# A smaller first place for the experts, and tokens fetched ahead of weights

## The chip, the cores and the metric

The kernel runs on one core of a Trainium2 chip. The metric is the device time of one execution in microseconds (us). Before the change the median of three timed runs is 489.94 us (487.93 to 490.13). The trace that is read below is of one more execution, which took 488.21 us.

## What is computed

Three stages follow each other: causal attention with a decay, for 2 batches of 8 heads and 576 positions; a mixture of eight experts, where each token goes to the expert with the highest logit and an expert takes at most 288 tokens; and one more two-layer network.

```python
x = attention(q, k, v, f)                 # 1152 tokens of 512
logits = x @ w_gate; expert_idx = np.argmax(logits, axis=1)
for i in range(N):                        # in order, at most 288 per expert
    e = expert_idx[i]
    if counts[e] < capacity: disp[e, counts[e]] = x[i]; ...
h = np.maximum(np.einsum('ecd,edf->ecf', disp, w1), 0.0)
y = np.einsum('ecf,efd->ecd', h, w2)
out[i] = gate_w[i] * y[expert_idx[i], pos[i]]
h2 = out @ w_in; g = piecewise(h2); return g @ w_out
```

With the inputs of these runs expert 0 gets 89 tokens and the other seven 69 to 288.

## The kernel before

**Attention** goes over 16 heads in steps of about 5 us. TensorE (PE) works on scores of one head and on the product with V of another; ScalarE (ACT) takes the exponentials into `pt`; GpSimd (POOL) masks their diagonal blocks (`affine_select`, L542), and PE's product with V (`av_part`, L579) needs the masked blocks. The order of each step is a list written by hand (`ORDER`).

**Dispatch.** `disp` in DRAM has E times `CAPS` rows: a slot per expert and position. SP fills it with zeros (L880), two transfers of 128 rows at the start of each step, 22 in all. From step 11 on POOL scatters the scaled token rows into it (L720, `scatter`): five scatters for the first batch, inside the last steps of attention, and five for the second batch after attention. `CAPS` is worked out from the table `PLACES`: the largest place but one with an overflow area `RW` behind it, where `RW` is the largest number of tokens by which an expert may exceed its place.

**Places.** The experts are not run by number, but by place: `PLACES` gives for each of the eight places the rank of the expert by its token count and the rows that the place computes. Place 0 is always expert 0, and its tokens don't come from `disp`: PE picks them with selection matrices (`pick` on VectorE (DVE), `perm` on PE, L712: ten token tiles by four column blocks, 40 products, each two records in the trace) straight into `XT`. What exceeds a place is done later under `tc.If` (`rest`); with these inputs no place is exceeded.

**One place** has 8 weight quarters of 512 KB: four of `w1`, four of `w2`. PE goes over 8 column blocks `fc` of `w1` (L1035 where the place has up to 160 rows, in plain fp32), and ACT's Relu (L1090) moves each from one of four PSUM banks into `hf`. Then the `w2` half follows in eight parts. Places over 160 rows (2, 4, 6) are "split": weights and tokens are made into a high and a low half first, and PE takes three products (L991 to L993). For place 2 the splitting of the tokens stands inside the `w1` loop of place 1: `x_trans` is called after blocks 1, 3, 5 and 7. Its DVE transpose (L1020) reads the fetched tokens, and its ACT copy (L1021) stands in ACT's queue ahead of the Relu of blocks 2 and 3.

**Loads.** All weights come over SP's queue in one order, `loads`; `pump` (L189) issues the next as soon as one of 13 buffers (8 `RAW`, 5 `ST`) is free. The eight quarters of place 0 are loaded in attention. `x_fetch(e)` puts four transfers (L400) for the tokens of place `e` into the same queue, out of `disp`, so it waits for the scatters. SP carries its list out in order.

Of the kernel before, what the change touches and what calls it, by code (L numbers as in the profile page):

```python
# [10 lines left out]
F32 = mybir.dt.float32  # L11
# [4 lines left out]
ACTF = mybir.ActivationFunctionType  # L16
# [8 lines left out]
def most_over(places, n):  # L25
    best = 0
    for m in range(1 << len(places)):
        over = [p for p in range(len(places)) if m >> p & 1]
        need = sum(places[p][1] + 1 for p in over if p == 0)
        for r in range(len(places) - 1):  # L30
            need += max([places[p][1] + 1 for p in over if p and places[p][0] >= r], default=0)
        if need <= n:
            best = max(best, len(over))
    return best
# [3 lines left out]
def attention_moe_mlp_kernel(  # L38
# [14 lines left out]
    nc = tc.nc  # L53
# [6 lines left out]
    KD = DM // 128  # L60
# [3 lines left out]
    KF = 8  # L64
# [1 line left out]
    NG = 3  # L66
    GW = N // NG
    GT = GW // 128
    PLACES = ((7, 160), (6, 128), (0, 288), (5, 128), (1, 224), (4, 128), (2, 192), (3, 160))
    CP = [c for _, c in PLACES]  # L70
    C0, CMAX = CP[0], max(CP)
    PS = [sum(CP[:p]) for p in range(E + 1)]
    LEFT = [min(cap, N // (r + 1) if p else N) - c for p, (r, c) in enumerate(PLACES)]
    RW = max(LEFT) // 32 * 32
    CAPS = max([c + RW for c, o in zip(CP, LEFT) if o > 0] + CP)
    NK = most_over(PLACES, N)
    XW = max([min(N, PS[p]) + CP[p] for p in range(E)] + [N + RW])
    THREE = 256
    SPLIT = [c > 160 for _, c in PLACES]
    NHL = 5  # L80
# [19 lines left out]
    xt_p = ctx.enter_context(tc.tile_pool(name="xtp", bufs=1))  # L100
# [25 lines left out]
    def build_consts(pos_c):  # L126
# [5 lines left out]
        for e in range(E):  # L132
            nc.gpsimd.memset(slot_c[:, e:e + 1], float(e * CAPS) - BIG)
            nc.gpsimd.memset(rev_c[:, e:e + 1], float(E - e))
            nc.gpsimd.memset(tie_c[:, e:e + 1], float(E - e if e else -E * N))
            nc.gpsimd.memset(place_c[:, e], float(PLACES[e][0]))
            nc.gpsimd.memset(cap_c[:, e:e + 1], float(CP[e]))
# [10 lines left out]
    def quarter_src(i):  # L148
        p, r = divmod(i, 8)
        w = (w1, w2)[r // 4]  # L150
        if p == 0:
            return w1[E, r] if r < 4 else w2[0, r - 4]
        return w[bass.ds(at_place(p), 1), r % 4].rearrange("e p f -> (e p) f")
# [3 lines left out]
    def at_place(p):  # L157
        if p not in places:
            places[p] = nc.sync.value_load(ord_i[0:1, p:p + 1], min_val=0, max_val=E - 1)
        return places[p]  # L160
# [18 lines left out]
    def pump(n=99):  # L179
        while n and free and loads:  # L180
            _, kind, i = loads.popleft()
            t = raws[kind, i] = free.popleft()
            if kind == "w":
                src = quarter_src(i)
            elif kind == "m":
                t, src = t.bitcast(U32), (w_in, w_out)[i % 2][i // 2].bitcast(U32)
            else:
                src = more_src(i)
            nc.sync.dma_start(out=t, in_=src)  # L189
            n -= 1  # L190
# [200 lines left out]
        nc.vector.tensor_tensor(out=order_sb, in0=ps[:, NT:], in1=ge[:, 0, 0:NT], op=ALU.add)  # L391

    xrs, xts, x_next = {}, {}, []
    XT = xt_p.tile([128, KD, C0], F32, tag="xt", name="XT")

    def x_load(e, src):
        n = src.shape[0] // 32
        xrs[e] = x_next[e % 2]
        for j in range(DM // 128):
            nc.sync.dma_start(out=xrs[e][32 * j:32 * j + 32, 0:n],  # L400
                          in_=src[:, 128 * j:128 * j + 128].rearrange("(t p) d -> p t d", p=32))


    with ExitStack() as actx:
# [303 lines left out]
        def perm(b, ibs, ks=range(KD)):  # L708
            for ib in ibs:
                n = min(128, S - ib * 128)  # L710
                for k in ks:
                    nc.tensor.matmul(px[k][:, 0:C0], xss[b][:n, ib, 2 * k:2 * k + 2].rearrange("p h d -> p (h d)"),  # L712
                                     sel[b, ib][:n].bitcast(F32), start=((b, ib) == (0, 0)),
                                     stop=((b, ib) == (NB - 1, IB - 1)))

        def scatter(b, ibs):
            si, xs = sis[b], xss[b]
            for ib in ibs:
                n = min(128, S - ib * 128)
                nc.gpsimd.indirect_dma_start(  # L720
                    out=disp_v[b * IB + ib], out_offset=bass.IndirectOffsetOnAxis(ap=si[:n, ib:ib + 1], axis=0),
                    in_=xs[:n, ib].rearrange("p h d -> p (h d)"), in_offset=None,
                    bounds_check=E * CAPS - 1, oob_is_err=False)
# [149 lines left out]
        for t in range(-AHD, NH + 1):  # L873
# [24 lines left out]
            if t == HB + 6:  # L898
                px = [next(s1), next(s1), next(s2), next(s2)]
# [21 lines left out]
        for k in range(KD):  # L921
            perm(1, range(3, IB), (k,))
        xts[0] = XT
        for k in range(KD):
            if k % 2:
                nc.vector.tensor_copy(out=XT[:, k], in_=px[k][:, 0:C0])
            else:
                nc.scalar.activation(out=XT[:, k], in_=px[k][:, 0:C0], func=ACTF.Copy)
        scatter(1, range(IB))
        bases_gen = compact_bases()  # L930

# [34 lines left out]
    def m_step(h):  # L966
        while m_at and m_at[0] <= h:
            m_at.pop(0)
            next(conv)
# [32 lines left out]
    with ExitStack() as mctx:  # L1002
        mp = mctx.enter_context(tc.tile_pool(name="moe", bufs=1))
        x_next.extend(mp.tile([128, max(CP[2 - i::2] + [RW]) // 32, 128], F32, name=f"xn_r{i}")
                      for i in range(2))
        xn = mp.tile([128, KD, 2, CMAX], F32R, name="xn")
        hf = mp.tile([128, KF, C0], F32, name="hf")
        xT0 = mp.tile([128, CMAX], F32, name="xT0")

        def x_trans(e, k, n, split):  # L1010
            if k == 0:
                xts[e] = xn if split else XT
            x = xts[e][:, k]
# [15 lines left out]
        def bank(ring, n, split):  # L1029
            t = next(ring)  # L1030
            return t[:, 0:n] if n >= THREE or not split else t[:, 0:2 * n].rearrange("p (z c) -> p z c", c=n)

        def product(ps, w, c, a, first, last):
            if len(a) == 1:
                nc.tensor.matmul(ps, w[:, c], a[0], start=first, stop=last)  # L1035
            elif len(ps.shape) == 2:
                three(ps, w[:, 0, c], w[:, 1, c], a[0], a[1], first, last)
            else:
                pair(ps, w[:, 0, c], w[:, 1, c], a[2], first, last)
# [40 lines left out]
        def more_src(i):  # L1080
            return (w1, w2)[i % 8 // 4][bass.ds(more_e[i // 8], 1), i % 4].rearrange("e p f -> (e p) f")

        pump()
        hx = mp.tile([128, KF, 2, CMAX], F32R, name="hx")
        tp = mctx.enter_context(tc.tile_pool(name="sum", bufs=2))
        invert = invert_slots(px[3][:, 32:32 + 2 * (N // 128)], tp)
# [37 lines left out]
        def x_fetch(e):  # L1124
            if e < E:
                x_load(e, disp.rearrange("(e c) d -> e c d", c=CAPS)[bass.ds(at_place(e), 1), 0:CP[e]]
                       .rearrange("e c d -> (e c) d"))

        for e in range(E):
            x, n, split = xts.pop(e), CP[e], SPLIT[e]  # L1130
            for r in range(4):
                i = e * 8 + r
                for fi in range(2):
                    fc = r * 2 + fi
                    ps = bank(ph_ring, n, split)
                    for k in range(KD):
                        c = slice(k * 256 + fi * 128, k * 256 + fi * 128 + 128)
                        product(ps, (hls if split else raws)["w", i], c, operand(x, k, n, split), k == 0, k == KD - 1)
                    hidden(ps, fc, n, split, 2 * i + fi)
                    w_step(2 * i + fi)  # L1140
                    if e + 1 < E and SPLIT[e + 1] and 2 * r + fi in XUP:
                        x_trans(e + 1, XUP.index(2 * r + fi), CP[e + 1], True)
                if i == 0:
                    x_fetch(1)
                if r == 3:
                    x_fetch(e + 2)
                extra(i)
                done("w", i)
            yb = {}
            for s, (d, f0, f1) in enumerate(PARTS):  # L1150
                i = e * 8 + 4 + d
                if f0 == 0:
                    yb[d] = bank(py_ring, n, split)
                for fc in range(f0, f1):
                    c = slice(fc * 128, fc * 128 + 128)
                    product(yb[d], (hls if split else raws)["w", i], c, operand(hx if split else hf, fc, n, split), fc == 0, fc == KF - 1)
                if f1 == KF:
                    token(yb[d], d, n, *bases[e])
                z = 2 * e * 8 + 8 + s
                w_step(z)  # L1160
                m_step(z)
                for k in range(KD):
                    if e + 1 < E and not SPLIT[e + 1] and s == XAT[k]:
                        x_trans(e + 1, k, CP[e + 1], False)
                if s % 2:
                    extra(z // 2)
                if f1 == KF:
                    done("w", i)
# [171 lines left out]
```

## Time and profile before

| | us |
|---|---|
| median of three runs | 489.94 (487.93 to 490.13) |
| the profiled execution | 488.21 |
| its span, first to last instruction | 486.5 |
| PE busy | 468.9 (96%) |
| DVE, ACT, POOL busy | 305.5, 256.6, 152.4 |

An engine's busy time says how much it worked, not whether it set the end. The timeline shows at which time an instruction began and in brackets how long its engine had stood idle before it, and for what. Windows show the busy time of an engine in a stretch, the granted clock of PE (1.00 is 2.4 GHz, 0.50 is 1.2 GHz), the share of the DMA engines and what they moved.

### The profile page before, as it was taken

The numbers are of one execution on the slowest core, as the hardware profiler recorded it, in microseconds if no ns is written. First come the engines' busy times: TensorE is split into PE (matmuls) and PEld (weight loads), VectorE is DVE, ScalarE is ACT, GpSimd is POOL, SyncE is SP. The second block draws the span as 40 slices with busy tenths as digits, with TensorE's granted clock in tenths as the row PEclk, the third lists the DMA queues.
The fourth block names the chain that finished last, engine by engine and source line by source line (L and its number), as shares of the span: only waits on it lengthen the run. The fifth ranks groups of instructions, "written<-read, shape, count | busy, mean of one in ns | idle before, by whom it ended". The sixth has DMA issues, their size and how long they took to land. (4 is left out here: it accounts for less than half of the span.)

```text
span 486.5 us, 8890 instructions
## 1 busy us (share of the span) xinstructions
PE 468.9 (96%) x3049; PEld 430.2 (88%) x3049; DVE 305.5 (63%) x779; ACT 256.6 (53%) x577; POOL 152.4 (31%) x256
## 2 busy tenths in 40 slices
PE   5899999999999999999999699999999999999995
PEld 2489998999899999999999699999999999999994
DVE  7776668844415757757664358787878554755532
ACT  7577777765223642663662344545445465566650
POOL 9587666763301380292190400000000000400002
PEclk8699999999999999999999889999999999999999
DMA  6468998821569995988960194344400000300001
GB/s 199 138 207 260 333 293 298 274 73 44 194 243 341 349 342 149 367 265 279 299 255 2 31 364 133 129 127 131 129 1 0 1 0 2 129 1 1 1 0 65
DMA packets 38576, 78.46 MB, mean 161 GB/s; under 512 B 14103, under 2 KB 19175, under 8 KB 38524
## 3 DMA queue, kind: packets, MB, share of 16 engines
q1 hardware_dynamic: 37020, 73.19, 45.7%
q0 software_dynamic: 1456, 4.57, 2.4%
q8 instruction: 26, 0.43, 0.4%
q14 instruction: 26, 0.21, 0.1%
q10 hardware_dynamic: 48, 0.06, 0.0%
HBM read 67.36 MB, written 10.49 MB: 160 GB/s over the span
## 5 line engine op out<-in xcount | busy, mean ns | idle before, releaser
L991 PE MATMUL PB<-x2h,HL 128*128 128x384 f32 x192 | 65.9, 343 | 3.9 <-DVEq L1207 3.9
L993 PE MATMUL PB<-x2h,HL 128*128 128x384 f32 x192 | 65.5, 341 | 0.0
L992 PE MATMUL PB<-x2l,HL 128*128 128x384 f32 x192 | 65.3, 340 | 0.0
L1247 DVE SCALAR_TENSOR_TENSOR PB<-PB,s 128x384 f32<-128x384 f32 x48 | 27.2, 566 | 54.9 <-ACT s L1245 54.9
L579 PE MATMUL PB<-VT,pt 128*128 128x102 f32 (+2 forms) x480 | 59.6, 259 | 0.0
L579 PEld LDWEIGHTS PB<-VT,pt 128*128 128x128 f32 (+2 forms) x480 | 54.1, 172 | 3.8
L1244 ACT ACTIVATE s<-PB 128x384 f32<-128x384 f32 x48 | 23.6, 491 | 62.8 <-PE PB L993 56.9
L1262 PE MATMUL PB<-HL,gh 128*128 128x512 f32 x144 | 56.6, 393 | 0.0
L1261 PE MATMUL PB<-HL,gh 128*128 128x512 f32 x144 | 56.4, 392 | 0.0
L1263 PE MATMUL PB<-HL,gl 128*128 128x512 f32 x144 | 56.0, 389 | 0.0
L1268 POOL DMA_INDIRECT out_dram<-ST,order_sb x6 | 6.0, 997 | 138.8 <-DVE ST L1267 137.9
L539 ACT ACTIVATE pt<-PB 128x288 f32<-128x288 f32 (+2 forms) x96 | 35.4, 390 | 22.8 <-PE PB L538 20.5
L505 DVE CUSTOM_DVE_ANT_0 dump<-PB,msk 128x128 f32<-128x128 f32 (+1 forms) x64 | 31.1, 489 | 21.5 <-PE PB L499 19.0
L991 PEld LDWEIGHTS PB<-x2h,HL 128*128 128x128 f32 x192 | 36.9, 192 | 5.9 <-issue 4.1
L1248 ACT ACTIVATE gh<-PB 128x384 fp32r<-128x384 f32 x48 | 23.6, 492 | 31.9 <-DVE PB L1247 31.9
L499 PE MATMUL PB<-KB,QM 128*128 128x128 f32 (+2 forms) x96 | 34.7, 372 | 5.6 <-DVE KB L775 3.6
L992 PEld LDWEIGHTS PB<-x2l,HL 128*128 128x128 f32 x192 | 36.8, 192 | 1.8
L993 PEld LDWEIGHTS PB<-x2h,HL 128*128 128x128 f32 x192 | 36.8, 191 | 0.0
L1250 DVE TENSOR_TENSOR gl<-PB,gh 128x384 fp32r<-128x384 f32 x48 | 26.8, 558 | 13.4 <-ACT gh L1248 13.4
L1263 PEld LDWEIGHTS PB<-HL,gl 128*128 128x128 f32 x144 | 27.1, 188 | 6.0
L988 DVE TENSOR_TENSOR HL<-wc,HL 128x512 fp32r<-128x512 f32 x40 | 27.0, 719 | 7.3 <-ACT HL L987 7.3
L1261 PEld LDWEIGHTS PB<-HL,gh 128*128 128x128 f32 x144 | 27.0, 188 | 4.4
(285 smaller groups left out, 1126.8 us busy)
## 6 DMA issues: line engine op xcount, KB each, us to landing
RAW<-in_w_dram SPq DMA_DIRECT2D x40, 512.0 KB
ST<-in_w_dram SPq DMA_DIRECT2D x24, 512.0 KB
qk<-in_qkT_dram SPq DMA_DIRECT2D x15, 576.0 KB
RAW<-in_w_in_dram SPq DMA_DIRECT2D x12, 512.0 KB
disp<-zero SPq DMA_DIRECT2D x22, 256.0 KB
RAW<-in_w_out_dram SPq DMA_DIRECT2D x9, 512.0 KB
ST<-in_w_out_dram SPq DMA_DIRECT2D x7, 512.0 KB
VT<-in_v_dram SPq DMA_DIRECT2D x8, 320.0 KB
```

What stands on the lines that cost most here:

```text
L499: nc.tensor.matmul(s[:n, :w - a], QM[h % 2][:, ib * 128:ib * 128 + n], KB[i][:, a:w], start=True, stop=True)
L505: nc.vector.tensor_tensor_reduce(out=dump[:n, :w - a], in0=s[:n, :w - a], in1=msk[:n, m0:m0 + w - a], scale=1.0, scalar=NEG if r < IB else ...
L539: nc.scalar.activation(out=pt[:n, POFF[jb] + a:POFF[jb] + z], in_=s[:n, :z - a], func=ACTF.Exp, scale=0.125)
L579: nc.tensor.matmul(o[:n, ib, ws], pt[:m, c0:c0 + n], v[:m, jb].rearrange("p a b -> p (a b)")[:, vs], start=(jb == 0), stop=(jb == ib))
L988: eng.tensor_tensor(out=w[:, 1, z], in0=c[:, s], in1=w[:, 0, z].bitcast(F32), op=ALU.subtract)
L991: nc.tensor.matmul(ps, wh, ah, start=first, stop=False)
L992: nc.tensor.matmul(ps, wh, al, start=False, stop=False)
L993: nc.tensor.matmul(ps, wl, ah, start=False, stop=last)
L1247: nc.vector.scalar_tensor_tensor(out=ps, in0=ps, scalar=1.0, in1=s, op0=ALU.max, op1=ALU.min)
L1261: nc.tensor.matmul(o, gh[:, c], wh, start=(fc == 0), stop=False)
L1262: nc.tensor.matmul(o, gh[:, c], wl, start=False, stop=False)
L1263: nc.tensor.matmul(o, gl[:, c], wh, start=False, stop=(fc == NF2 - 1))
```

## The change

The place of expert 0 shrinks from 160 to 128 rows, and with it the selection, its products, and the two products with the weights. Two tiles that other places share keep 160 columns (`CF`). `RW` grows from 128 to 160, so `CAPS` from 352 to 384 and `disp` from 2816 to 3072 rows. Besides, the fetch of the tokens of place 1 moves from inside the loop of place 0 to ahead of the loop, and ahead of `pump`, which loads place 1's first five weight quarters.

```diff
-    PLACES = ((7, 160), (6, 128), (0, 288), (5, 128), (1, 224), (4, 128), (2, 192), (3, 160))
+    PLACES = ((7, 128), (6, 128), (0, 288), (5, 128), (1, 224), (4, 128), (2, 192), (3, 160))
-    C0, CMAX = CP[0], max(CP)
+    C0, CMAX, CF = CP[0], max(CP), max(c for c in CP if c <= 160)
...
-    XT = xt_p.tile([128, KD, C0], F32, tag="xt", name="XT")
+    XT = xt_p.tile([128, KD, CF], F32, tag="xt", name="XT")
...
-                nc.vector.tensor_copy(out=XT[:, k], in_=px[k][:, 0:C0])
+                nc.vector.tensor_copy(out=XT[:, k, 0:C0], in_=px[k][:, 0:C0])
...
-                nc.scalar.activation(out=XT[:, k], in_=px[k][:, 0:C0], func=ACTF.Copy)
+                nc.scalar.activation(out=XT[:, k, 0:C0], in_=px[k][:, 0:C0], func=ACTF.Copy)
...
-        hf = mp.tile([128, KF, C0], F32, name="hf")
+        hf = mp.tile([128, KF, CF], F32, name="hf")
...
-        pump()
         hx = mp.tile([128, KF, 2, CMAX], F32R, name="hx")
...
+        x_fetch(1)
+        pump()
         for e in range(E):
...
-                if i == 0:
-                    x_fetch(1)
                 if r == 3:
                     x_fetch(e + 2)
```

On SP, at the end of attention, `disp` has two more blocks of zeros; they come at the start of step 12. Ahead of them stands the V load of that step, behind them the small transfer of head 15 (`QB<-ct`):

```order
 L460 DMA VT_160<-in_v_dram 128x10x64 [waits DMAHW7_49,PE_49]
-L516 DMA QB_152<-ct 1x5x128 [waits DMAHW0_49,Activation_49]
+L880 DMA disp<-zero 128x512 [waits DMAHW0_49,DMASW0_49]
+L880 DMA disp<-zero 128x512 [waits DMAHW1_49]
+L516 DMA QB_152<-ct 1x5x128 [waits DMAHW2_49,Activation_49]
```

DMASW0 is the semaphore of POOL's first scatter, DMAHW0 and DMAHW1 those that the two new transfers raise. The first new transfer stands behind the landing of the first scatter, and the transfer of head 15 behind both.

On POOL, at the same place, the second scatter; behind it stand the copy of the gate columns into V (L464) and the masks of head 14:

```order
 L542 AFFINE_SELECT pt<-pt 64x64 [waits Activation_49]
-L720 DMA disp<-xs,si 2816x512 [waits Activation_49]
+L720 DMA disp<-xs,si 3072x512 [waits DMAHW1_49,DMAHW0_49,Activation_49]
 L464 COPY VT_160<-vwall 128x10x8
 L542 AFFINE_SELECT pt<-pt 128x128 [waits Activation_49] x4
```

The second scatter has two new waits, for the two blocks of zeros.

On SP, from the start of the experts, before the change (`ST` and `RAW` are weight buffers, `xn_r` the fetched tokens; 32x4 are the 128 of place 1, 32x9 the 288 of place 2):

```order
L189 DMA ST_1761<-in_w_dram 128x1024
L189 ISA
L189 DMA ST_1762<-in_w_dram 128x1024
L400 ISA
L400 DMA xn_r_1789<-disp 32x4x128
...
L189 DMA RAW_100<-in_w_dram 128x1024
L189 ISA
L189 DMA RAW_101<-in_w_dram 128x1024
L189 DMA RAW_102<-in_w_in_dram 128x1024
L159 TENSOR_LOAD ord_i
L159 ISA x2
L400 ISA
L400 DMA xn_r_1788<-disp 32x9x128
```

and with it:

```order
L400 DMA xn_r_1791<-disp 32x4x128
L189 ISA
L189 DMA ST_1760<-in_w_dram 128x1024
...
L189 DMA ST_1764<-in_w_dram 128x1024
L189 ISA
L189 DMA RAW_100<-in_w_dram 128x1024
L189 ISA
L189 DMA RAW_101<-in_w_dram 128x1024
L189 DMA RAW_102<-in_w_in_dram 128x1024
L159 TENSOR_LOAD ord_i
L159 ISA x2
L400 ISA
L400 DMA xn_r_1790<-disp 32x9x128
```

The five `ST` loads stood ahead of the first token fetch and now stand between it and the three `RAW` loads, and so between the two token fetches.

## Rows read from the trace of the kernel before

**Rows 1.** The page's slices of the span: PE busy, and its granted clock.

```profile
PE   5899999999999999999999699999999999999995
PEclk8699999999999999999999889999999999999999
```

**Rows 2.** PE in five stretches: length, busy time (records), granted clock, DMA share, GB/s.

```profile
117.10:130.20 13.10, 12.98 (x80) 1.00 0.24 72
130.20:139.00 8.80, 8.79 (x64) 1.00 0.83 325
139.00:147.70 8.70, 8.70 (x66) 1.00 0.72 231
147.70:155.00 7.30, 7.30 (x66) 1.00 1.06 324
155.00:162.33 7.33, 7.33 (x67) 1.00 1.04 395
```

**Rows 3.** POOL's timeline at steps 11 to 13: start, length, instruction, idle before it.

```profile
100.21 1.17 POOL L720 DMA_INDIRECT disp<-xs,si  x1 [0.30 <-POOL QB L487]
104.31 0.99 POOL L720 DMA_INDIRECT disp<-xs,si  x1 [0.60 <-ACT ct L515]
105.28 0.29 POOL L464 COPY VT<-vwall 128x80 f32<-128x80 f32 x1
105.49 0.78 POOL L542 TENSOR_SCALAR_AFFINE_SELECT pt<-pt 128x128 f32<-128x128 f32 x2
```

**Rows 4.** The scatter at 100.21 by itself, from its start to its landing.

```profile
DMA to landing us min/median/max: 5.3/5.3/5.3
```

**Rows 5.** One 512 KB load on an empty queue: SP's timeline, and a window behind it.

```profile
187.06 0.35 SPq L189 DMA_DIRECT2D RAW<-in_w_dram  x1
...
190.00:191.00 1.00, 1.00 (x12) 1.00 0.42 41
```

**Rows 6.** PE's timeline at step 14: the first product with V of head 14.

```profile
109.17 0.36 PE L579 MATMUL PB<-VT,pt 128*128 128x102 f32 x2
```

**Rows 7.** The four scatters that follow the first in attention, start and landing.

```profile
L720 POOL DMA_INDIRECT disp<-xs,si x4: 918/987/996, 104.3 to 115.4; - x4
...
DMA to landing us min/median/max: 2.2/2.8/3.0
```

**Rows 8.** The five scatters behind attention, start and landing.

```profile
L720 POOL DMA_INDIRECT disp<-xs,si x5: 912/972/974, 125.9 to 131.0; - x5
...
DMA to landing us min/median/max: 6.5/7.6/8.2
```

**Rows 9.** SP's timeline at the start of the experts.

```profile
125.59 2.55 SPq L189 DMA_DIRECT2D ST<-in_w_dram  x5
138.91 1.89 SPq L400 DMA_DIRECT2D xn_r<-disp  x4
141.06 0.96 SPq L189 DMA_DIRECT2D RAW<-in_w_dram  x2
...
143.30 1.88 SPq L400 DMA_DIRECT2D xn_r<-disp  x4
```

**Rows 10.** DVE's timeline: the transpose of place 2's tokens, in place 1.

```profile
151.72 0.70 DVE L1020 STREAM_TRANSPOSE xT<-xn_r 128x288 f32<-128x288 f32 x1 [2.25 <-DMA xn_r<-disp]
```

**Rows 11.** ACT's timeline there: Relu of block 1, the copy, Relu of blocks 2 and 3.

```profile
149.75 0.28 ACT L1090 ACTIVATE hf<-PB 128x128 f32<-128x128 f32 x1 [0.62 <-PE PB L1035]
152.45 0.44 ACT L1021 ACTIVATE xn<-xT 128x288 fp32r<-128x288 f32 x1 [2.43 <-DVE xT L1020]
152.80 0.42 ACT L1090 ACTIVATE hf<-PB 128x128 f32<-128x128 f32 x2
```

**Rows 12.** Two windows of PE and the DMA engines, columns as in Rows 2.

```profile
143.00:145.00 2.00, 2.00 (x17) 1.00 1.02 412
145.00:151.60 6.60, 6.60 (x57) 1.00 1.03 269
```

**Rows 13.** PE behind the experts: its timeline, and windows.

```profile
278.94 0.66 PE L991 MATMUL PB<-x2h,HL 128*128 128x384 f32 x1 [3.88 <-DVEq L1207]
...
275.00:278.00 3.00, 0.06 (x1) 0.86 0.04 11
...
279.00:284.00 5.00, 5.00 (x16) 0.50 0.97 376
284.00:285.00 1.00, 1.00 (x8) 0.99 1.08 430
```

## The prediction

> **What bounds the kernel now.** I read the page's slices first: PE is busy in nearly every slice from the second on, at full clock, with dips only at the start and behind the experts [rows 1]. Then I read PE stretch by stretch through the places that the change touches: the selection for place 0, its two halves, then the two halves of place 1. PE has no gap in any of them [rows 2]. So PE sets the end, and a shorter place 0 should be a gain one for one, provided that what follows is ready earlier too. That is the question that the rest of the views answer: who arrives just in time? The reader should look at four queues: POOL at the end of attention, SP at the start of the experts, and DVE and ACT inside place 1.
>
> **What the smaller place gives.** Per record PE needs 8.80 / 64 = 0.1375 us with 160 rows and 7.30 / 64 = 0.114 us with 128 [rows 2]; the difference is 0.0234 us. (The counts 66 and 67 include records that overlap a window's edge; each half has 64.) Selection: 80 records, 1.9 us less. First half of place 0: 8.80 - 7.30 = 1.5 us. Second half: 8.70 - 7.33 = 1.4 us. Together 4.8 us. The narrower selection masks, copies and Relus lie on DVE and ACT beside PE's work and count as nothing; without that cover they would be a gain of a few tenths, never a loss.
>
> **What the longer `disp` costs in attention.** The two new blocks of zeros wait for the first scatter, which starts at 100.21 [rows 3] and lands 5.3 us later [rows 4], at 105.5. SP then issues both within about 1 us. A 512 KB load on an empty queue, as much as both together, starts at 187.06 and moves its last bytes just after 190 [rows 5], 3 us. So the zeros land at about 108.8. POOL's second scatter, until now at 104.31 [rows 3], waits for them, and POOL takes its queue in order: scatter 1.0 us, copy of the gate columns 0.3, first mask 0.3 [rows 3], which makes 110.6 to 110.7. PE wants this mask at 109.17 [rows 6]. I take a stall of **1.5 us**. Its bounds are 0 (the zeros land 1.5 us sooner) and 2.5 (1 us later). The later masks come every 0.3 us and are not late; head 15's small transfer on SP moves from 104 to behind the zeros and is wanted at 109.0, within the same stall. In attention PE has no gap in which to take the 1.5 us back.
>
> So place 1 would begin on PE at 147.7 - 4.8 + 1.5 = 144.4 [rows 2], and its first six blocks, 0.91 us each, end at 149.9.
>
> **What the moved fetch does.** Before, five weight loads went out at 125.59 [rows 9], at the same time as the five scatters, which then took 6.5 to 8.2 us to land, where the scatters without such company took 2.2 to 3.0 [rows 7, 8]. The last started at 131.0 and landed at 138.6, and SP's first token fetch went out at 138.91 [rows 8, 9]. Now the scatters have the queue to themselves. They begin at 125.9 + 1.5 - 0.6 (24 of the 80 shorter records stand ahead of the routing) = 126.8, the last at 131.9, landed at 134.5; the fetch goes out at 134.8, **4.1 us earlier**. Place 1's tokens are there by 138.5, and its first weights, issued at 137, by 140, against 144.4: both hidden, with some 4 us to spare.
>
> The tokens of place 2 are another matter. Between the two fetches there were three loads; now there are eight. At the 412 GB/s of a full queue [rows 12] a 512 KB load takes 1.28 us, five take **6.4 us**. So place 2's tokens land at 151.7 - 4.1 + 6.4 = 154.0. Who waits for them? DVE did already: its transpose stood idle 2.25 us for this transfer and began at 151.72 [rows 10]. ACT's copy of it began at 152.45 after 2.43 us of waiting, and behind it in ACT's queue stood the Relus of blocks 2 and 3, at 152.80 [rows 11]. These free the PSUM banks that PE's blocks 6 and 7 write. The first of them ended at 153.1, and block 6, six blocks behind 147.7, was due at 147.7 + 5.5 = 153.2: before, the chain was just in time, with no slack. With the change block 6 goes at 154.0 + 1.5 = 155.5, though PE would be ready at 149.9. The whole gain of 3.3 us is eaten there, and PE is **2.3 us later** than before from block 6 on. What follows hangs on the same tokens and on PE, which has hardly a gap up to the end of the experts [rows 1], so the delay stays.
>
> **The clock.** PE would stand idle 5.6 us before block 6. Behind the experts it stands idle 3.88 us, and the granted clock falls while it does (0.86 over 275 to 278) and stays at 0.50 for the first 5 us of work [rows 13]. I take the same here: 5 us at 1.2 GHz do half the work, **2.5 us** lost. Bounds: nothing, and 5 us if it stayed low twice as long.
>
> **Sum.** -4.8 + 1.5 + 5.6 (wait for the tokens) + 2.5 = +4.8 us on the profiled execution's own 488.2: **493.0 us**. The median of the runs shown is 1.7 us above that execution, which the range has to allow for.
>
> A rule to weigh against this: before, from 143.0 to 151.6 the queue moved 2 x 412 + 6.6 x 269 = 2600 KB [rows 12], but the three loads and the tokens are about 2160, of which some 130 had gone already. About 570 KB of later loads overtook the tokens, worth 570 / 269 = 2.1 us. The Trainium skill (DMA: Bandwidth & Descriptors, "Queues, rings and completion order") has each DMA engine consume the descriptors of a ring in ring order; by that the tokens would fall behind nothing that was issued after them. The trace differs, since later loads did move first. With eight loads ahead of them, all issued long before, the tokens may queue more strictly; then they land 2.1 us sooner, at 151.9.
>
> **The rivals.**
> - *Strict order.* Tokens at 151.9, block 6 at 153.4, 0.2 us later than before; idle 3.5 us, so the clock still falls: +2.7, **490.9 us**. For it: the arithmetic above. Against it: the overtaking was there when three loads stood ahead. Chance 0.15, half of it on either side of the 0.5% line.
> - *The clock holds.* Everything else as forecast: +2.3, **490.5 us**. Against it: 3.88 us of idleness were enough once [rows 13]. Chance 0.15.
> - *Other side, the tokens come in time.* If they land by 148.4, ACT's copy is never in the way of block 6, and the gain of 4.8 less 1.5 stands: **485.0 us**. It decides at 148.4; that needs them 5.6 us earlier than I work out, so neither the POOL stall (1.5) nor the overtaking (2.1) alone would do it, and the eight loads cannot take less than 10.2 us at the rate of rows 12. Chance 0.07.
>
> **How the numbers follow.** The forecast has a chance of 0.63. A measurement of this kernel can tell about 0.5%, 2.4 us, from no change. Slower by more: 0.63 + 0.07 = 0.70. Within: 0.15 + 0.08 = 0.23. Faster: 0.07. The range goes from 488.0 (strict order with a clock that holds) to 497.0 (the forecast with the longer stall, or the clock low for longer, and the 1.7 us between median and profile); it leaves out the faster rival and a tail above.
>
> **What would show it.** Right: a PE gap of 1 to 2 us at the first product with V of head 14, with POOL's second scatter near 109; scatters behind attention that land in about 3 us; SP's first fetch near 134.8; DVE's transpose for place 2 waiting for its DMA until about 154; a PE gap of over 5 us inside the first half of place 1; a granted clock of 0.50 behind it. Wrong: PE without a gap in place 1 (then the tokens came in time), or a gap with the clock at 1.00. If PE waits at place 1's first matmul instead, its weights are what is late.

## The result, and the profile after

The changed kernel takes 494.1 us (median of 11 runs, 492.1 to 496.1), the kernel before 489.0 beside it (11 runs, 487.1 to 492.4). The ratio is 1.010, with a 95% interval of 1.008 to 1.012: **slower by 5.1 us**, where +4.8, to 493.0, had been forecast. The profiled execution of the changed kernel took 496.1 us (span 494.4); it is the slowest of the eleven, 2 us over their median. It reaches the first scatter 1.32 us later than the profile of before (101.53 against 100.21). Steps are therefore compared from that scatter on, and what is special to this one execution is said below.

The smaller place first. PE's timeline in the changed kernel, from the selection (whose first row stands here) to place 2; columns are start, length, instruction, count, and in brackets the idle time before it:

```profile
119.68 1.97 PE L712 MATMUL PB<-QB,xs 128*128 128x128 f32 x16
...
130.82 7.41 PE L1035 MATMUL PB<-XT,RAW 128*128 128x128 f32 x64
138.07 7.31 PE L1035 MATMUL PB<-hf,RAW 128*128 128x128 f32 x64
145.22 5.52 PE L1035 MATMUL PB<-XT,ST 128*128 128x128 f32 x48
159.76 3.78 PE L1035 MATMUL PB<-XT,ST 128*128 128x128 f32 x16 [9.01 <-ACT hf L1089]
...
171.13 0.38 PE L991 MATMUL PB<-xn,HL 128*128 128x288 f32 x1
```

The selection takes 130.82 - 119.68 = 11.14 us and the halves of place 0 take 7.41 and 7.31, against 13.10, 8.80 and 8.70 [rows 2]: 1.96 + 1.39 + 1.39 = **4.74 us less**. Place 1 begins at 145.22, which is 2.5 us earlier than before in spite of the late start. Then block 6 waits 9.01 us, and blocks 6 and 7 take 3.78 us where 16 records at full clock take 2.05 (a row of the order-alone experiment below).

POOL at the end of attention, and the PE product that waits there:

```profile
101.53 1.16 POOL L720 DMA_INDIRECT disp<-xs,si  x1 [0.29 <-POOL QB L487]
110.09 0.99 POOL L720 DMA_INDIRECT disp<-xs,si  x1 [5.04 <-ACT pt L539]
111.06 0.28 POOL L464 COPY VT<-vwall 128x80 f32<-128x80 f32 x1
```

```profile
111.64 0.47 PE L579 MATMUL PB<-VT,pt 128*128 128x102 f32 x2 [0.96 <-POOL pt L542]
```

The second scatter begins 8.6 us after the first, where it began 4.1 us after it [rows 3], and PE waits 0.96 us for the mask.

SP at the start of the experts:

```profile
106.56 0.82 SPq L880 DMA_DIRECT2D disp<-zero  x2
...
135.92 1.92 SPq L400 DMA_DIRECT2D xn_r<-disp  x4
138.03 2.47 SPq L189 DMA_DIRECT2D ST<-in_w_dram  x5
140.77 0.92 SPq L189 DMA_DIRECT2D RAW<-in_w_dram  x2
141.80 0.77 SPq L189 DMA_DIRECT2D RAW<-in_w_in_dram  x1
143.40 4.27 SPq L400 DMA_DIRECT2D xn_r<-disp  x4
147.91 8.22 SPq L189 DMA_DIRECT2D RAW<-in_w_dram  x5
```

The first token fetch goes out 3.0 us earlier than before (138.91 [rows 9]), or 4.3 counted from the first scatter. Of the five scatters behind attention the trace has the landing of the last one alone; it took 2.7 us (the five before: 6.5 to 8.2 [rows 8]):

```profile
DMA to landing us min/median/max: 2.7/2.7/2.7
```

The five `ST` loads go out at 138.03 instead of 125.59, and the second fetch at the same time as before (143.40 against 143.30) with five more loads ahead of it. Who waits for it, on DVE and on ACT:

```profile
154.94 0.43 DVE L953 TENSOR_SCALAR wc<-RAW 128x512 uint32<-128x512 uint32 x1 [8.49 <-DMA RAW<-in_w_in_dram]
...
158.38 0.68 DVE L1020 STREAM_TRANSPOSE xT<-xn_r 128x288 f32<-128x288 f32 x1 [3.01 <-DMA xn_r<-disp]
```

```profile
147.27 0.28 ACT L1089 ACTIVATE hf<-PB 128x128 f32<-128x128 f32 x1 [0.62 <-PE PB L1035]
159.09 0.44 ACT L1021 ACTIVATE xn<-xT 128x288 fp32r<-128x288 f32 x1 [11.55 <-DVE xT L1020]
159.44 0.42 ACT L1089 ACTIVATE hf<-PB 128x128 f32<-128x128 f32 x2
```

Read from the bottom: the Relus of blocks 2 and 3 (159.44) stand behind the copy (159.09), which waits for DVE's transpose (158.38), which waits for the tokens. That is the forecast chain, place by place [rows 10, 11]. What the forecast did not have is the row above the transpose: DVE first waits 8.49 us for the first load of the last network's weights, called the gate weights below (`w_in`, the third `RAW` load on SP). Its conversion stands in DVE's queue ahead of the transpose. So two waits in a row hold PE, called the two gates below: first the gate weights, then the tokens.

The windows of PE in that stretch: length, busy time (records), granted clock, share of the DMA engines, GB/s:

```profile
145.00:150.00 5.00, 5.00 (x47) 1.00 1.02 410
150.00:152.00 2.00, 0.74 (x7) 1.00 1.17 223
152.00:154.00 2.00, 0.00 (x0) 1.00 1.14 197
154.00:156.00 2.00, 0.00 (x0) 0.66 1.02 319
156.00:158.00 2.00, 0.00 (x0) 0.50 1.02 370
...
162.00:166.00 4.00, 4.00 (x26) 0.64 0.94 321
```

The clock falls to 0.50 (1.2 GHz) inside the wait and is back only within 162 to 166. And the queue, which moved 410 GB/s over 145 to 150, moves 197 to 223 while most of the tokens' small rows (512 bytes, 128 floats) go through, at no smaller share of the DMA engines.

The packets of the DMA engines show more of this wait. Place 2's tokens are 1152 rows of 512 bytes; the count under 2 KB less the count under 512 B is the rows. First 149 to 153, then 153 to 157, in the changed kernel:

```profile
DMA packets 1239, 1.01 MB, mean 252 GB/s; under 512 B 75, under 2 KB 1128, under 8 KB 1238
DMA packets 413, 1.20 MB, mean 301 GB/s; under 512 B 35, under 2 KB 132, under 8 KB 412
```

and in the order-alone experiment below (run 2), whose first fetch goes out at the same time (135.96):

```profile
DMA packets 1344, 1.05 MB, mean 262 GB/s; under 512 B 80, under 2 KB 1232, under 8 KB 1344
DMA packets 414, 1.53 MB, mean 383 GB/s; under 512 B 44, under 2 KB 44, under 8 KB 412
```

In run 2 all 1152 rows are through by 153. In the changed kernel's profile 1053 are; the other 99 trail until 157.1, beside weight loads that SP issued later, and the tokens count as landed only with the last row. What holds these rows back was not settled. Run 6 below loads in the same order too, and there DVE's transpose began 20.0 us after the fetch of place 1's tokens, not 22.5 as here.

From the first scatter to place 2's first product the kernel before needs 162.33 - 100.21 = 62.1 us, the changed one 171.13 - 101.53 = **69.6**, and the smaller place without any wait would need 62.1 - 4.7 = **57.4**. From place 2 to the end both take nearly the same (324.2 and 323.3 us). The stretch from the first scatter to place 2 is the yardstick of the experiments.

### The profile page after: what moved, and what is told of

Its sections match the earlier page's. It is cut to its first block, busy times and chain, and to the rows that moved or that the text cites. A ratio compares the mean times of both kernels' runs of the same rounds, so it can differ in the third digit from the quotient of the medians.

```text
span 494.4 us, 8893 instructions
## 1 busy us (share of the span) xinstructions
PE 465.8 (94%) x3049; PEld 427.3 (86%) x3049; DVE 306.6 (62%) x779; ACT 255.9 (52%) x577; POOL 152.0 (31%) x256
```

## The experiments

Twelve kernels were run, each against the kernel before on the same chip (489.1 to 489.8 us in these batches). Edits are shown against the changed kernel. Theory A is the forecast's: the moved fetch puts five loads ahead of place 2's tokens, and the wait for them with the clock's fall outweighs the smaller place.

**1. The smaller place alone** (old order of the loads).

```diff
-        x_fetch(1)
-        pump()
+        pump()
         for e in range(E):
...
+                if i == 0:
+                    x_fetch(1)
```

> The place of 128 rows with the loads in the old order (five weight loads, then the tokens of place 1). Theory A (place 2's tokens gate block 6 of place 1 through ACT's queue, and PE's wait makes the clock fall): the scatters begin 0.9 us later than before (1.5 of stall less 0.6), so place 2's tokens land at about 152.6, block 6 begins near 154, PE idle some 4 us, clock at 0.50 behind it: before + 0.9 + 2.5, about 492.4 us. Rival B (only the new order of the loads costs, the smaller place by itself gains its 4.8 us less the stall of 1.5): about 485.7 us, no PE gap in place 1.

Measured: 489.2 us, ratio 1.000 (0.998 to 1.003). Both expectations fall. PE in its profile:

```profile
112.04 0.47 PE L579 MATMUL PB<-VT,pt 128*128 128x102 f32 x2 [1.37 <-POOL pt L542]
146.34 2.05 PE L1035 MATMUL PB<-hf,RAW 128*128 128x128 f32 x16 [2.32 <-DVE x2l L1117]
154.70 2.05 PE L1035 MATMUL PB<-XT,ST 128*128 128x128 f32 x16 [0.95 <-ACT hf L1090]
```

The 4.7 us are given back in three waits: 1.37 in attention, 2.32 at the end of place 0, 0.95 in place 1, together 4.64 (yardstick 62.4). The second is new, and DVE shows where it comes from:

```profile
145.15 0.69 DVE L1016 STREAM_TRANSPOSE XT<-xn_r 128x128 f32<-128x128 f32 x2 [12.10 <-DMA xn_r<-disp]
```

DVE waits for place 1's tokens, and behind that transpose in its queue stand the evictions of place 0. The scatters land as slowly as before (7.6 and 8.1 us for the two whose landing is in the trace), so SP's fetch goes out at 141.19. So the loads' old order was just in time at two places, for place 1's tokens and for place 2's, and a PE that arrives 4.7 us sooner waits at both.

**2. The moved fetch alone.**

```diff
-    PLACES = ((7, 128), (6, 128), (0, 288), ...
+    PLACES = ((7, 160), (6, 128), (0, 288), ...
```

> The new order of the loads with 160 rows; disp keeps 22 blocks of zeros. Theory A: no stall in attention; the last scatter lands at about 133.6, place 2's tokens at 151.7 - 5.0 + 6.4 = 153.1, block 6 at 154.6 against 153.2 before: 1.4 us later, a gap too short for the clock: about 490.4 us; if the tokens are overtaken by later loads as in the changed kernel's trace, 3 us more and a fall of the clock, up to 495. Rival B' (the order costs nothing while PE is not early): 489 us, no gap.

Measured: 490.6 us, ratio 1.004 (1.002 to 1.007), as theory A has it. PE comes to block 6 some 4 us later here than in the changed kernel, and the tokens come sooner: DVE's transpose begins at 153.78, or 52.2 us behind the first scatter, against 56.8 in the changed kernel's profile and 53.1 to 54.5 in runs 3, 5 and 6. So they cost PE only half a microsecond, at full clock:

```profile
155.18 2.05 PE L1035 MATMUL PB<-XT,ST 128*128 128x128 f32 x16 [0.54 <-ACT hf L1089]
```

```profile
153.78 0.70 DVE L1020 STREAM_TRANSPOSE xT<-xn_r 128x288 f32<-128x288 f32 x1 [2.45 <-DMA xn_r<-disp]
```

Neither half of the change alone costs 1%. Together they do, since the one half brings PE sooner to the spot at which the other half has made the tokens later.

**3. The zeros earlier**: the two new blocks at step 0 instead of step 12, so that the second scatter does not wait.

```diff
-            for z in range(2 * t - 2, 2 * t):
+            for z in (range(22, 24) if t == 0 else range(2 * t - 2, min(2 * t, 22))):
```

> The changed kernel with the last two blocks of zeros written at step 0 instead of step 12, so that they wait for no scatter. Theory A: the PE gap of about 1 us at head 14's product with V goes, and everything behind it, the second scatters and place 2's tokens too, comes 1 to 1.5 us earlier: 492.6 to 493.1 us. Rival C (the stall is hidden under the later wait for the tokens): 494.1 us, unchanged.

Measured: 493.6 us, ratio 1.010 (1.007 to 1.013): between the expectations. The wait in attention is gone (the second scatter follows the first 4.1 us later, as before the change). The median falls by 0.5 us against the changed kernel's 494.1, which the intervals don't tell from nothing. PE waits 6.55 us at block 6:

```profile
155.11 3.79 PE L1035 MATMUL PB<-XT,ST 128*128 128x128 f32 x16 [6.55 <-ACT hf L1089]
```

**4. Place 2's tokens ahead of the weights**: `x_fetch(2)` right behind `x_fetch(1)`.

```diff
         x_fetch(1)
+        x_fetch(2)
         pump()
```

> The changed kernel with the fetch of place 2's tokens right behind that of place 1, ahead of the weights. Theory A, with what the trace of the changed kernel adds (DVE's first conversion of a w_in chunk stands ahead of the transpose in DVE's queue and waits for the eighth load): tokens land near 142 to 146, but DVE waits for that load until about 153.5, so block 6 comes near 155: 2 to 3 us less than the changed kernel, about 491.5 us, with DVE's long wait put down to the w_in load. Rival D (the tokens' landing is the only gate): PE has no gap at block 6, no fall of the clock, about 486 us.

Measured: 493.4 us, ratio 1.008 (1.005 to 1.012). The transpose no longer waits for tokens, and yet it starts only at 155.75, since the gate weights hold DVE:

```profile
155.41 0.43 DVE L953 TENSOR_SCALAR wc<-RAW 128x512 uint32<-128x512 uint32 x1 [8.73 <-DMA RAW<-in_w_in_dram]
155.75 0.67 DVE L1020 STREAM_TRANSPOSE xT<-xn_r 128x288 f32<-128x288 f32 x1
```

**5. The gate weights later**: the first conversion at block 4 of place 1 at the earliest, instead of block 0, and so its load some places later.

```diff
-lambda h: h >= 16 and h % 16 in MRES[SPLIT[h // 16]]
+lambda h: h >= 20 and h % 16 in MRES[SPLIT[h // 16]]
```

> The changed kernel, with the first conversion of the gate weights put from block 0 of place 1 to block 4 or later, so that DVE does not wait for that load ahead of the first transpose of place 2. Theory A (both gates bind, the tokens last: 158.4 us in the profile, the gate weights 154.9 us): DVE now waits for the tokens alone, they land between 156 and 158 us, PE waits 5.5 to 9 us before block 6, and the time stays at 493 to 494. Rival B (the gate weights alone bind, and the tokens are on time when they are not behind them): the wait falls to under 2 us and the time to 487 to 488.

Measured: 494.8 us, ratio 1.010 (1.008 to 1.013), as theory A. Now DVE waits for the tokens alone, just as long:

```profile
156.03 0.68 DVE L1020 STREAM_TRANSPOSE xT<-xn_r 128x288 f32<-128x288 f32 x1 [9.32 <-DMA xn_r<-disp]
```

PE waits 6.15 us at block 6 in run 4 and 6.41 in run 5. Each gate by itself holds it.

**6. PE kept busy in the wait**: 32 products of ones, never read, ahead of block 6.

```diff
+                    if (e, fc) == (1, 6):
+                        for _ in range(32):
+                            nc.tensor.matmul(px[3][:, 0:512], ones_b, ones_b.unsqueeze(1).to_broadcast([128, 4, 128]),
+                                             start=True, stop=True)
```

> Adds 32 products of ones (512 columns each, never read) on PE ahead of block 6 of place 1, where PE stands idle for 9.0 us in the changed kernel's profile. They bring no token and no weight earlier: DVE's transpose still starts when the tokens have landed (157 to 159 us). Theory A (the wait is one price, and the fall of the granted clock behind it is another, about 2.5 us): the granted clock stays at 1.00 through the wait and behind it, the 64 products of blocks 6 and 7 take as long as those ahead of them, and the time falls by 2 to 2.5 us, to 491.5 to 492. Rival B (the clock costs little, since what follows waits for data anyway): the time stays within 0.5 us of the changed kernel's 494.1. Rival C: the idle products push out block 6 themselves: slower than the changed kernel.

Measured: 492.0 us, ratio 1.006 (1.004 to 1.008). Theory A holds: 2.1 us less than the changed kernel, for products that compute nothing. (The two ratios, 1.006 and 1.010, come from separate batches, and their intervals touch.)

```profile
149.26 7.07 PE L1138 MATMUL PB<-ones_b 128*128 128x512 bf16 x32
156.17 1.95 PE L1035 MATMUL PB<-XT,ST 128*128 128x128 f32 x16
```

```profile
154.00:156.00 2.00, 2.00 (x11) 1.00 1.01 401
```

```profile
154.55 0.69 DVE L1020 STREAM_TRANSPOSE xT<-xn_r 128x288 f32<-128x288 f32 x1 [2.83 <-DMA xn_r<-disp]
```

Block 6 comes 6.9 us behind the six blocks ahead of it here, 6.55 us in run 3; with the clock at 1.00 the 16 records take 1.95 us and not 3.79. Place 2's tokens come 20.0 us after the fetch of place 1's here (SP's fetch is at 134.56).

**7. Both gates taken away** (edits of 4 and 5 together).

> The changed kernel with both gates taken away: place 2's tokens are fetched right behind place 1's, ahead of all further weights, and the first conversion of the gate weights comes at block 4 of place 1 or later. Zeros and scatters stay as in the changed kernel. Theory A (the two loads in front of DVE's first transpose of place 2 are the whole of the loss; the smaller place does gain 4.8 us): no wait over 1 us at block 6 of place 1, the clock stays at 1.00 there, PE waits about 1 to 1.4 us once in attention for POOL's mask, and the time is 485.0 to 486.5. Rival D (the weights that now come later hold up place 0 or place 1 in their stead): PE waits for a weight load somewhere in the first two places and the time is above 488.5.

Measured: 492.9 us, ratio 1.008 (1.005 to 1.010). Theory A falls, and rival D comes close: the blocks of `w1` run without a wait, but PE then waits in the `w2` half of place 1.

```profile
161.26 1.22 PE L1035 MATMUL PB<-hf,ST 128*128 128x128 f32 x4 [6.29 <-ACT hf L1089]
```

```profile
158.14 0.43 DVE L953 TENSOR_SCALAR wc<-RAW 128x512 uint32<-128x512 uint32 x1 [8.69 <-DMA RAW<-in_w_in_dram]
```

It is the gate weights again, now four blocks later in DVE's queue, and behind them another transpose of place 2's tokens.

**8. Both gates and the zeros** (edits 3 and 5, and place 2's fetch behind two weight loads). In this run and in 10 to 12 the zeros are moved as in run 3, to step 0; where an expectation has "one step earlier", that edit is meant.

```diff
         x_fetch(1)
+        pump(2)
+        x_fetch(2)
         pump()
```

> As the kernel that takes both gates away, but place 2's tokens are fetched behind two weight loads, and the two zero blocks that the first scatter waits for in the changed kernel are written one step earlier, so that POOL is not held up in attention. Theory A: no PE wait over 0.5 us between 90 and 170 us, and the time is 484.2 to 485.5, about 1 us under the kernel with both gates taken away and 3.5 to 4.8 us under the kernel before. Rival D (a later wait takes the gain as it did where the smaller place stood alone): above 487.

Measured: 492.3 us, ratio 1.007 (1.005 to 1.010): rival D. PE stands once for 6.37 us at the same spot as in run 7. So the order among the loads is not the whole cause: in runs 4, 5, 7 and 8 PE waits 6.2 to 6.4 us for whichever of them it needs last. The new theory E looked at what stands ahead of all of them, SP's wait for the scatters, during which the free `ST` buffers stay empty.

**9. Three weight loads ahead of the first fetch.**

```diff
+        pump(3)
         x_fetch(1)
         pump()
```

> The changed kernel, with three weight loads (1.57 MB) ahead of place 1's token fetch and the rest behind it; nothing else differs. Theory E (the loss is a hole of about 10 us in the loads: SP sits on the token fetch, which waits for the scatters, while the weights' places are free from 125 us on; all that is loaded behind it then comes that much later at about 410 GB/s): the DMA engines move about 1.5 MB more before 136 us, the gate weights and place 2's tokens land 3 to 4 us earlier than in the changed kernel, the wait at block 6 of place 1 falls from 9.0 or 6.5 us to 2 to 4, the clock may hold, and the time falls to 489 to 491.5. Rival A (the order of the loads, not the hole, sets when tokens and gate weights land): the same loads stand ahead of place 2's tokens, so they land as late, and the time stays at 493 to 494. Rival S (three loads slow the scatters as five do, 7.6 to 8.2 us to land): place 1's fetch goes out at 139 to 141 and a wait of 1 to 2 us for place 1's tokens comes back.

Measured: 493.1 us, ratio 1.008 (1.005 to 1.012). Mixed. More is moved early, as E has it, and the gate weights come at 149.28, 49.1 us behind the first scatter (53.4 in the changed kernel's profile). But the scatters slow down with it (rival S): SP's fetch goes out at 137.90, or 37.7 us behind the first scatter (34.4 in the changed kernel), the hole comes back behind the three loads, and place 2's tokens come no sooner (53.9 us behind the first scatter).

```profile
137.90 1.88 SPq L400 DMA_DIRECT2D xn_r<-disp  x4
```

```profile
130.00:135.00 5.00, 5.00 (x48) 1.00 1.00 381
135.00:140.00 5.00, 5.00 (x47) 1.00 0.17 55
```

(In the changed kernel these windows hold 186 and 80 GB/s.) PE waits 0.48 us for place 1's tokens and 5.27 at block 6; the time is that of rival A.

**10 and 11. The same with the other edits**: three weight loads, place 1's tokens, two loads, place 2's tokens, the rest, with edits 3 and 5 (first); three loads, both token fetches, the rest, with edit 3 (second).

```diff
+        pump(3)
         x_fetch(1)
+        pump(2)
+        x_fetch(2)
         pump()
```

(The second is without the `pump(2)`.)

> The smaller place with this order on SP: three weight loads, place 1's tokens, two weight loads, place 2's tokens, the rest; the first conversion of the gate weights at block 4 of place 1 or later; the last two zero blocks one step earlier. Theory E (hole in the loads): the three loads ahead win back about 3.8 us for everything behind them, which is most of the 6.4 us that PE waited for the gate weights in the kernel with all three other edits; the wait falls to 1 to 3 us, the clock holds, and the time is 486 to 488.5, under the kernel before. Rival A (order alone): as the kernel with all three other edits, 492.3. Rival S (the scatters slow down as behind five loads): a wait of 1 to 2 us at place 1's tokens, 489 to 490.

> As the last, but place 2's tokens come right behind place 1's and the first conversion of the gate weights stays at block 0 of place 1, with its load as the eighth. Theory E: the gate weights' load moves up by the three loads ahead and lands at 149 to 151 us instead of 155; DVE then takes the transposes without a wait for tokens; PE waits 0 to 3 us at block 6 of place 1; 485.5 to 488.5. Rival A: gate weights as late as before, wait of 5 to 6 us, 492 to 493. Rival S: a wait for place 1's tokens of 1 to 2 us, 488 to 490.

Measured: 491.7 us, ratio 1.005 (1.003 to 1.007), and 490.7 us, ratio 1.004 (1.001 to 1.006). Both lie between E and A in time, below the changed kernel and slower than before. The waits are nearer to A's: PE waits 0.42 us for place 1's tokens and 5.07 for the gate weights in the first, 0.60 and 4.68 in the second.

**12. All five loads ahead, as before the change**, with edits 3 and 5 and both token fetches together inside the loop.

```diff
+        pump()
...
                 if i == 0:
                     x_fetch(1)
+                    x_fetch(2)
```

> The smaller place with the loads of the kernel before: all five weight loads go out ahead of place 1's tokens, so there is no hole in the loads. Three edits are added: the last two zero blocks one step earlier (no wait in attention), place 2's tokens right behind place 1's, and the first conversion of the gate weights at block 4 of place 1 or later. The smaller place with the old order alone stood at 489.2 and waited 1.4 us in attention, 2.3 for place 1's tokens and 0.95 for place 2's. Theory E (the smaller place's 4.8 us are there, and each of these three waits can be taken out by itself as long as the loads have no hole): the first and the third wait go, the second stays (2 to 2.7 us, the scatters still land 7.6 to 8.2 us after their issue beside five loads), the clock stays at 1.00, and the time is 486.5 to 488.0. Rival A (the loads as a whole are the limit here, so a wait taken out comes back at the next load): a new PE wait of 1.5 us or more for the gate weights at the end of place 1, and 488.5 to 490.

Measured: 489.3 us, ratio 1.000 (0.997 to 1.002). The time is rival A's, but the wait that A expected for the gate weights is only 0.24 us. The waits are as theory E has them: those in attention and for place 2's tokens are gone, the one for place 1's tokens stays. But the clock falls in it, which was not expected, and the time is not below the kernel before:

```profile
143.31 3.39 PE L1035 MATMUL PB<-hf,RAW 128*128 128x128 f32 x16 [2.28 <-DVE x2l L1117]
```

```profile
143.00:144.00 1.00, 0.69 (x5) 0.89 1.09 219
144.00:145.00 1.00, 1.00 (x7) 0.50 1.15 197
```

```profile
135.00:140.00 5.00, 5.00 (x48) 1.00 0.45 173
140.00:145.00 5.00, 2.72 (x20) 0.88 0.75 170
```

The last two windows show that the hole is there even with five loads ahead: the five `ST` buffers are full, and the loads into `RAW` wait on SP behind the token fetch, which goes out at 138.17. Its yardstick is 61.4 us against 57.4 without a wait: 2.3 for the tokens, 0.2 for the gate weights, and the rest, about 1.4, put down to the clock. Of the 0.8 us that it leads the kernel before at place 2, its profiled execution keeps 0.3 at the end, and the medians show none.

| kernel | us | first scatter to place 2, us | PE waits, us |
|---|---|---|---|
| before | 489.0 | 62.1 | none |
| changed | 494.1 | 69.6 | 0.96, 9.01 |
| 1 place alone | 489.2 | 62.4 | 1.37, 2.32, 0.95 |
| 2 order alone | 490.6 | 62.8 | 0.54 |
| 3 zeros early | 493.6 | 66.1 | 6.55 |
| 4 place 2's tokens first | 493.4 | 66.7 | 1.22, 6.15 |
| 5 gate weights later | 494.8 | 66.8 | 1.21, 6.41 |
| 6 PE kept busy | 492.0 | 65.0 | 0.99 (the one at block 6 is filled) |
| 7 both gates | 492.9 | 66.7 | 1.05, 6.29 |
| 8 both gates, zeros | 492.3 | 66.2 | 6.37 |
| 9 three loads first | 493.1 | 66.1 | 1.00, 0.48, 5.27 |
| 10 mixed order, later gate weights, zeros | 491.7 | 64.1 | 0.42, 5.07 |
| 11 three loads, both fetches, zeros | 490.7 | 64.5 | 0.60, 4.68 |
| 12 five loads first | 489.3 | 61.4 | 2.28, 0.24 |

No kernel of this study beats the kernel before. All orders of the loads that were tried share one thing: SP waits for the scatters with weights behind it. That this hole is the cause of the last 5 to 6 us is argued, not shown: runs 9 to 11 filled a part of it and stand 1.0 to 3.4 us below the changed kernel, two of them with other edits besides. A version in which the token fetch stands on another queue than the weights was not tried, and whether the smaller place is worth its 4.7 us there stays open.

## Why the prediction was right

**The time** came out right, 494.1 against 493.0 and +5.1 against +4.8, and by the mechanism forecast. One gate was missed, and one reading behind the tokens' time does not hold.

- *The smaller place, -4.8*: measured -4.74.
- *The stall in attention, +1.5*: measured 0.96 in the profile, 0.99 to 1.37 in other kernels with late zeros. The steps of the forecast (108.8, then 1.0, 0.3 and 0.3) add up to 110.4 and not to 110.6 or 110.7, which makes a stall of 1.2. Taking it out (run 3) gave no more than 0.5 us of time; fetch and tokens came about 1.2 us earlier with it, counted from the first scatter, but PE still waited 6.55 us at block 6.
- *The earlier fetch*: forecast at 134.8, which is 34.6 us behind the first scatter; measured 34.4. The landing of the last scatter, 2.6 us in the forecast, took 2.7.
- *The tokens of place 2*: forecast at 154.0, 19.2 us behind the fetch of place 1's tokens. From that fetch to DVE's transpose it took 19.8 to 20.0 us in runs 3, 5 and 6, 17.8 in run 2 and 22.5 in the changed kernel's profile, all with eight loads between the two fetches. So the term was right to within 1 us in three of these five, and the profile's late tokens belong to the slowest execution. That a spread of 17.8 to 22.5 has the forecast in its middle is in part luck. The premise that some 570 KB of later loads overtake the tokens does not hold as it was read: the bytes were counted up to 151.6, but the last row began at 150.8, and some 330 KB had gone ahead by then. In run 2 the queue moved 16.98 us x 303 GB/s = 5145 KB from the first fetch to the last row; both fetches and the eight loads make 5046 KB, so hardly anything overtook. Run 2's 17.8 us is close to the 17.1 of the rival of a strict order; in the others it is the last rows that come late. The Trainium skill (DMA: Bandwidth & Descriptors, "Queues, rings and completion order") states the order for each engine's ring, and says in the same place that completion is not in order for the issuing engine as a whole. The trace agrees with both: 1053 of the 1152 rows went in one block behind the loads, and 99 trailed beside later ones.
- *The wait at block 6, +5.6*: measured 9.0 in this execution, 6.2 to 6.6 in runs 3 to 5, whose medians are within 0.7 us of the changed kernel's. The chain (transpose, copy, Relu, PSUM bank, PE) was right. That the gate weights stand ahead in DVE's queue and come only some 3 us sooner was not in the forecast. It did not change the time, since without them DVE waits as long for the tokens (run 5); but it is why run 4 failed to gain.
- *The clock, +2.5*: 69.6 - 57.4 - 0.96 - 9.01 = 2.2 us, and run 6 gave back 2.1.

The rival in which the tokens come in time had the gain at 485.0 us. Run 1 shows that even a kernel without the moved loads does not get there, since three waits, 4.64 us in all, take its place.

## What to carry to other kernels

Before an engine is made faster in one stage, look for each consumer that now waits a little or arrives just in time (here DVE's 2.25 us for tokens at full PE): the gain ends there unless the supply is moved by as much. A transfer that waits for others, put at the head of a list that is carried out in order, holds back all that is ready behind it; read what the free buffers could have been filled with meanwhile. And when the profiled execution is the slowest of its kernel, look for the same step in another run before its size is explained. When two edits are bundled, time each alone: here one was worth nothing, the other cost 0.4%, and together they cost 1%.

## What the runs showed of the hardware that was not expected

- While most of the rows of 512 bytes went through (150 to 154 in the changed kernel), the queue moved 197 to 223 GB/s at a share of 1.14 to 1.17, against 410 at 1.02 just before.
- With the same eight loads between the two fetches, DVE's transpose of place 2's tokens began 17.8 to 22.5 us after the first fetch went out: 135.96 to 153.78 in run 2, 133.74 to 153.74 in run 3, 136.22 to 156.03 in run 5, 134.56 to 154.55 in run 6, 135.92 to 158.38 in the changed kernel.
- A PE wait of 2.28 us was enough for the granted clock to fall to 0.50 in run 12; waits of 2.32 and 0.95 us in run 1 left it at 1.00, as its windows behind the two waits show (below). What makes the difference was not settled. Idle products of ones in the wait kept it at 1.00 in run 6.
- The last of the five scatters lands in 2.7 us alone (the changed kernel) and in 7.6 beside five weight loads (run 1), although it began 2.8 us after the last of these had been issued (130.46, the scatter at 133.28).

```profile
146.40:148.00 1.60, 1.60 (x14) 1.00 1.02 387
155.00:157.00 2.00, 2.00 (x20) 1.00 1.03 412
```
